# Sparse attention feeding a squared-ReLU MLP on one core: batches 2 to 4 loaded by casting DMAs with long rows, their local q and k transposed on TensorE

## The chip, the cores and the metric

The kernel runs on one core of a Trainium2 chip. A core has TensorE (PE: matmuls, with its weight loads shown as PEld), VectorE (DVE), ScalarE (ACT), GpSimd (POOL), and SyncE (SP), which here only issues DMAs. The metric is the device time of one execution in microseconds; several executions are taken and their median is given.

## What is computed

Attention over 8 batches of 8 heads, 576 positions and 64 channels. Heads 0 to 3 are local (a query sees itself and the 31 positions before it), heads 4 to 7 are strided (it sees earlier positions with the same remainder modulo 32). The result, with heads side by side, is a matrix of 4608 tokens by 512, and goes through an MLP with a squared ReLU:

```python
scores = scale * np.matmul(q, k.transpose(0, 1, 3, 2))
scores = np.where(masks[None, :, :, :], scores, -1000000000.0)
attn = np.exp(scores - np.max(scores, axis=-1, keepdims=True))
attn = attn / (np.sum(attn, axis=-1, keepdims=True) + 1e-09)
x = np.matmul(attn, v).transpose(0, 2, 1, 3).reshape(B * S, H * D)
...
r = np.maximum(x @ w_in, 0.0)
return (r * r) @ w_out
```

## The kernel before

**Work and tiles.** The unit of attention is a pair of heads of one batch: unit u is batch u // 4, pair u % 4; the first two pairs are local, the last two strided. A local unit needs only band blocks (96 queries against 128 keys), a strided one only the blocks of equal remainder (72 by 72). All operands of TensorE are bf16. The attention result is kept transposed in four tiles `xt`, [128 channels, 4608 tokens]. The MLP works on nine chunks of 512 tokens. For a chunk c, `mm1(c, ff)` is four 512-column matmuls into a "ph" bank, a Relu on ACT (L478) and a square on DVE (L481) into `g_sb`; `mm2(c, i)` is four 512-column matmuls (L495) of the second product, and every fourth one copies a finished [128, 512] tile (L499) and stores it through SP (L503). PSUM has eight banks: two "ph", one "py", five "pt".

**Steps of a unit.** T (`step_T`, L284) transposes local q or k on TensorE, six 96-column products, and copies q on ACT (L297) and k on DVE (L299). S (`step_S`, L333) makes the scores into four "pt" banks; ACT exponentiates them bank by bank (L343), DVE multiplies by the 0/1 mask (L349). Without `at_once` the four exponentials and two masks are spread over the next ticks, one per group, by `later`. D (`step_D`, L418) multiplies by V, whose 65th column of ones gives the sum, and DVE divides (L430, L431); a local unit has two parts, a strided one three. E (`step_E`) brings x into `xt`: by a DMA transpose on SP for local units from batch 2 on (L441), else by TensorE transposes (L448) and a copy (L454, L456). Batches 0 and 1 have their own forms for strided units: TS transposes q and k on TensorE (L186), N sums over keys by a product with ones (L381), O multiplies by V and DVE scales into `xt` (L394, L396).

**Order.** The schedule is written by hand. `first_steps` does batch 0 and the first five products of chunk 0. Then a list of groups is built, one group being one `mm1` or one `mm2` quarter: groups 0 to 15 chunk 0 first product (0 to 4 are empty), 16 to 31 its second product, 32 to 47 `mm1(1)`, 48 to 63 `mm2(1)`, 64 to 79 `mm1(2)`, and from 80 on `mm1(c)` and `mm2(c - 1)` in turn, 32 groups per chunk. Batch 1's steps are hung on groups 12 to 31 by `second(n, ...)`. The steps of batches 2 to 7 stand in one list (`stream_steps`), and `due` spreads each batch's steps over a stretch of groups in proportion to `weights`: batch 2 ends at group `ready[2]` = 56, batch b from 3 on at `starts[b]`, the first group of chunk b. A step that is due is issued ahead of its group on every engine, so each engine's queue is in this order, and an instruction that waits holds up all behind it on its engine.

**Loads.** Batches 0 and 1 and the weights come by casting DMAs issued from POOL (`load_qk_local_sw`, `load_v_local_sw`, `load_v_str_first`, `load_w_in`, `load_w_out`), which write bf16. From batch 2 on `loads(b)` issues on SP plain loads of local q and k (L118 for batches under `LB` = 4, else L112), local V (L210) and strided V (L242) in fp32, and POOL casts them (L140, L217, L218, L249). Strided q and k go by a casting DMA from POOL to DRAM (`cast_str_dram`, L163) and come back by a DMA transpose on SP (`transpose_str`, L171). For batches from `LB` on local q and k are transposed by DMA on SP too (`transpose_local`, L198) rather than by T. Batch 2's loads hang on group 18 and are held by a one-element POOL copy (L117) that reads the last part of `w_out_b`; batch 3's hang on group 34, and those of later batches are placed by `plan`. Staging tiles for q and k have two buffers each, the tiles for V four slots that batches use in turn.

The lines that fix the stretches and the loads of batches 2 and 3:

```python
weights.append(3 if c < 3 else 5)        # L688, mm1
weights.append(7 if c < 2 else 5)        # L691, mm2
ready = {2: 56}                          # L714
plan(2, 18, 0, 0)                        # L761
plan(3, 34, 0, 0)                        # L763
```

Of the kernel before, what the change touches and what calls it, by code (L numbers as in the profile page):

```python
# [14 lines left out]
def kernel(  # L15
# [18 lines left out]
    NJ = 8  # L34
# [67 lines left out]

    LB = 4

    def load_qk_local(u, eng, gate=None):
        b, p = units[u]
        s = st.setdefault(u, {})
        for name, src in (("q", q), ("k", k)):
            t = qk_st.tile([QL, 2, 6 * D], FP32, name=f"{name}_st")
            if b >= LB:  # L110
                for hh in range(2):
                    eng.dma_start(out=t[:, hh].rearrange("p (t d) -> p t d", d=D),  # L112
                                  in_=src[b, 2 * p + hh].rearrange("(t p) d -> p t d", p=QL))
                s[name + "f"] = t
                continue
            if gate is not None and name == "q":
                nc.gpsimd.tensor_copy(t[0:1, 0, 0:1], gate)  # L117
            eng.dma_start(out=t, in_=src[b, 2 * p:2 * p + 2]  # L118
                          .rearrange("h (p j) d -> p h (j d)", j=6))
            s[name + "f"] = t  # L120
# [35 lines left out]

    XB = 2
    big = {}

    def cast_str_dram(b):  # L160
# [7 lines left out]
    def transpose_str(b):  # L168
        for name in "qk":
            o = strT.tile([128, NJ // 2, 4 * SP_], BF16, name=f"{name}T_s")  # L170
            nc.sync.dma_start_transpose(out=o, in_=big.pop((b, name)))  # L171
            for i in range(2):
                st.setdefault(4 * b + 2 + i, {})[name + "T"] = o[:, :, 2 * SP_ * i:2 * SP_ * (i + 1)]
# [85 lines left out]

    clock = [0]  # L260
    pending = []

# [42 lines left out]
    def step_S(u, at_once=False):  # L305
# [57 lines left out]
        expo(0, 0)  # L363
        later(1, lambda: expo(0, 1), u)
        later(2, lambda: (masks(0), expo(1, 0)), u)
        later(3, lambda: expo(1, 1), u)
        later(4, lambda: masks(1), u)
# [66 lines left out]
    def step_E(u):  # L434
# [3 lines left out]
        local = is_local(u)  # L438
        n, w = (NL, QL) if local else (NJ, SP_)
        if local and b >= XB:  # L440
            nc.sync.dma_start_transpose(  # L441
                out=xt[p][:, b * S:(b + 1) * S].rearrange("c (t q) -> c t q", q=QL),
                in_=x.rearrange("p n d -> p (n d)"))
            st.pop(u)
            return
# [18 lines left out]
    def mm1(c, ff, kks=range(4), order=range(4), pool=None):  # L464
# [3 lines left out]
        if kks[0] == order[0]:  # L468
            phs[ff] = banks["pt"].pop(0) if pool == "pt" else bank(pool or "ph")
        ph = phs[ff]  # L470
# [8 lines left out]
        if c == 0 and 2 < ff < NP:  # L479
            banks["pt"].insert(0, ph)  # L480
        later(1, lambda: nc.vector.tensor_tensor(g[:, ff, :], r, r, op=ALU.mult))  # L481
# [3 lines left out]
    def mm2(c, i, pool=None):  # L485
        j, part = divmod(i, 4)
        g = gs[c]
        if part == 0:
            if pool == "pt":
# [15 lines left out]
    T_ = lambda u, nm: (lambda: step_T(u, nm))  # L505
    S_ = lambda u, at_once=False: (lambda: step_S(u, at_once))
    D_ = lambda u, part: (lambda: step_D(u, part))
# [34 lines left out]
    def stream_steps(lo, hi, base):  # L542
        order = [T_(lo, "q"), T_(lo, "k"), T_(lo + 1, "q"), S_(lo), T_(lo + 1, "k")]
        ends = {}
        for u in range(lo, hi + 1):
            if u < hi - 1:
                order.append(S_(u + 1))
            if u > lo:
                order.append(E_(u - 1))
                ends[u - 1] = base + len(order)  # L550
            if u < hi:
                order.append(D_(u, 0))
                if u + 2 < hi and has_T(u + 2):
# [9 lines left out]

    gates = {2: w_out_b[0:1, 12, 0:1]}

    def loads_1():
# [8 lines left out]
        load_w_out(3)  # L575
        for t in vl_sts:
            nc.gpsimd.memset(t[0:32], 0.0)

    def loads(b):
        u = 4 * b  # L580
        for i in range(2):
            load_qk_local(u + i, nc.sync, gate=gates.get(b) if i == 0 else None)
        for i in range(2):
            load_v_local(u + i, nc.sync)
        load_v_str(u + 2, nc.sync)
        load_v_str(u + 3, nc.sync)
        if b >= XB:
            cast_str_dram(b)
        cast_qk_local(u, pool2)
        cast_qk_local(u + 1, pool2)  # L590
        cast_v_local(u)
        cast_v_local(u + 1)
        cast_v_str(u + 2)
        cast_v_str(u + 3)

    def loads_qk(b):
        for i in range(2):
            load_qk_local(4 * b + i, nc.sync)
        cast_str_dram(b)
# [80 lines left out]
    def add(c, kind, i, pool=None):  # L680
# [3 lines left out]
        elif kind == 1:  # L684
            if i == 0:
                starts[c] = len(groups)
            groups.append(lambda: mm1(c, i))
            weights.append(3 if c < 3 else 5)  # L688
        else:
            groups.append(lambda: mm2(c, i, pool))  # L690
            weights.append(7 if c < 2 else 5)  # L691

# [6 lines left out]
    for part in range(4):  # L699
        for j, pool in ((0, "ph"), (1, "ph"), (2, None), (3, "pt")):  # L700
            add(0, 2, 4 * j + part, pool)
    mm1_alone(1)
    for i in range(16):
        add(1, 2, i, "ph")
# [8 lines left out]
    due = [0] * (len(groups) + 1)  # L713
    ready = {2: 56}  # L714
    hooks = {}
# [3 lines left out]

    def plan(b, n0, g0, g1):  # L720
        if b < LB:
            at(n0, lambda: loads(b))
            if b >= XB:
                at(n0 + (12 if b == 2 else 6), lambda: transpose_str(b))
            return
        g = g0 + (g1 - g0) * 45 // 100
        at(g, lambda: loads_qk(b))
        at(max(g + 8, g0 + (g1 - g0) * 8 // 10), lambda: transpose_str(b))
        at(n0, lambda: loads_v(b))
        for i in range(2):  # L730
            at(g + 14 + 4 * i, lambda u=4 * b + i: transpose_local(u))

# [9 lines left out]
    N_, O_ = (lambda u: lambda: step_N(u)), (lambda u: lambda: step_O(u))  # L742
    second(12, lambda: cast_qk_local(4, dve2, "q"))
    second(13, T_(4, "q"), lambda: cast_qk_local(4, dve2, "k"))
    second(14, T_(4, "k"), lambda: cast_qk_local(5, dve2, "q"))
    second(15, T_(5, "q"), lambda: cast_qk_local(5, dve2, "k"))
    second(16, T_(5, "k"))
    second(17, S_(4, True))
    second(19, S_(5, True))
    second(20, D_(4, 0))  # L750
    second(21, D_(4, 1), ts("q", 0))
    second(22, ts("q", 1), D_(5, 0))
    second(23, E_(4), D_(5, 1))
    second(24, ts("k", 0), ts("k", 1))
    second(25, E_(5))
    second(26, S_(6, True))
    second(28, S_(7, True), N_(6))
    second(29, O_(6))
    second(30, N_(7))
    second(31, O_(7))  # L760
    plan(2, 18, 0, 0)  # L761
    done_prev, g_prev = 0, 32
    plan(3, 34, 0, 0)  # L763
    for b in range(2, B):
        g_end, s_end = ready.get(b, starts[b]), ends[4 * b + 3]
        total = sum(weights[g_prev:g_end])
        for g in range(g_prev, g_end + 1):
            due[g] = done_prev + (s_end - done_prev) * sum(weights[g_prev:g]) // total
        if b + 2 < B:
            plan(b + 2, g_end + 2, g_prev, g_end)  # L770
        done_prev, g_prev = s_end, g_end
    done = 0
    for n, g in enumerate(groups):
        while done < due[n]:
            steps[done]()
            done += 1
# [36 lines left out]
```

The softmax here doesn't subtract the row's maximum and nothing guards it: scores larger than these inputs give would overflow.

## Time and profile before

| | |
|---|---|
| median of 8 runs | 319.03 us (318.19 to 319.97) |
| profiled execution, its own time | 319.91 us |
| span of its trace | 318.2 us |
| granted TensorE clock | 0.999 |
| DMA, mean over the span | 136 GB/s, 43.41 MB |
| hardware queue (SP), share of 16 engines | 44.5% |
| software queue (POOL), share | 23.0% |

The costliest groups of instructions, as the page gives them (busy time in us, then the mean of one in ns):

| line | engine, what | count | busy | mean |
|---|---|---|---|---|
| L472 | PE, first product | 549 | 141.5 | 379 |
| L495 | PE, second product (py and ph) | 534 | 137.1 | 379 |
| L478 | ACT, Relu | 141 | 84.0 | 598 |
| L481 | DVE, square | 144 | 67.3 | 469 |
| L343 | ACT, exponential | 128 | 48.0 | 407 |
| L431 | DVE, scale of x | 68 | 36.0 | 509 and 554 |
| L349 | DVE, mask | 56 | 30.6 | 588 and 504 |

How to read it: a matmul's duration (379 ns) is longer than the distance to the next one, since matmuls are pipelined, so PE's busy share overstates and its holes are found from start times. Some matmul records are missing (549 of 564 L472 rows into "ph"). In the rows of slices a digit is the busy share in tenths of one fortieth of the span, 7.95 us. In the chain of waits each piece is what released the next one, from the last instruction back. Idle time of ACT, DVE or POOL costs nothing by itself.

### The profile page before, as it was taken

The numbers are of one execution on the slowest core, as the hardware profiler recorded it, in microseconds if no ns is written. First come the engines' busy times: TensorE is split into PE (matmuls) and PEld (weight loads), VectorE is DVE, ScalarE is ACT, GpSimd is POOL, SyncE is SP. The second block draws the span as 40 slices with busy tenths as digits, with TensorE's granted clock in tenths as the row PEclk, the third lists the DMA queues.
The fourth block names the chain that finished last, engine by engine and source line by source line (L and its number), as shares of the span: only waits on it lengthen the run. The fifth ranks groups of instructions, "written<-read, shape, count | busy, mean of one in ns | idle before, by whom it ended". The sixth has DMA issues, their size and how long they took to land.

```text
span 318.2 us, 6089 instructions
## 1 busy us (share of the span) xinstructions
PE 300.4 (94%) x2319; PEld 148.4 (47%) x2362; DVE 163.4 (51%) x398; ACT 164.5 (52%) x339; POOL 83.1 (26%) x108
## 2 busy tenths in 40 slices
PE   8899699989899989999999999999999999999994
PEld 3544354444455444444444444544444444444441
DVE  5366653569766875755565557464455222222200
ACT  3757455777446765554555455545543344444311
POOL 8653213718820822831363024000000000000000
PEclk9999999999999999999999999999999999999999
DMA  8999979999998997998796575100421100000121
GB/s 158 164 205 205 190 132 261 214 255 221 235 143 195 190 248 170 240 191 209 182 216 146 139 180 99 39 25 31 54 66 50 37 33 35 33 33 35 52 80 66
DMA packets 87052, 43.41 MB, mean 136 GB/s; under 512 B 72112, under 2 KB 79984, under 8 KB 86832
## 3 DMA queue, kind: packets, MB, share of 16 engines
q1 hardware_dynamic: 73520, 31.86, 44.5%
q0 software_dynamic: 13504, 11.17, 23.0%
q8 instruction: 18, 0.29, 0.4%
q14 instruction: 10, 0.08, 0.1%
HBM read 37.08 MB, written 12.98 MB: 157 GB/s over the span
## 4 chain that ended last, share of the span: by engine, by line
PE 88%; DVE 5%; ACT 3%; issue 2%; ACTq 0%; DVEq 0%
PE ph L472 35%; PE py L495 27%; PE ph L495 10%; PE pt L418 4%; PE pt L333 4%; PE py L514 2%; ACT r L478 2%; PE pt L448 1%; DVE xt L456 1%; PE pt L495 1%; ACT e L343 1%; PE pt L284 1%; DVE g_sb L481 1%; DVE e L349 1%; DVE kTl L299 1%
## 5 line engine op out<-in xcount | busy, mean ns | idle before, releaser
L472 PE MATMUL ph<-xt,w_in_b 128*128 128x512 bf16 x549 | 141.5, 379 | 3.3 <-DVE xt L456 1.9
L478 ACT ACTIVATE r<-ph 128x512 bf16<-128x512 f32 x141 | 84.0, 598 | 100.3 <-PE ph L472 95.7
L481 DVE TENSOR_TENSOR g_sb<-r 128x512 bf16<-128x512 bf16 x144 | 67.3, 469 | 105.8 <-ACT r L478 105.3
L495 PE MATMUL py<-w_out_b,g_sb 128*128 128x512 bf16 x380 | 99.7, 379 | 1.6 <-issue 0.6
L495 PEld LDWEIGHTS <-g_sb 128*128 128x128 bf16 x576 | 52.8, 98 | 60.4 <-issue 3.1
L472 PEld LDWEIGHTS <-w_in_b 128*128 128x128 bf16 x576 | 51.6, 98 | 54.0 <-issue 0.8
L343 ACT ACTIVATE e<-pt 72x288 bf16<-72x288 f32 (+1 forms) x128 | 48.0, 407 | 14.6 <-PE pt L333 14.4
L495 PE MATMUL ph<-w_out_b,g_sb 128*128 128x512 bf16 x154 | 37.4, 379 | 0.3
L418 PEld LDWEIGHTS <-e 128*128 128x128 bf16 (+1 forms) x384 | 20.1, 97 | 15.6 <-issue 1.9
L217 POOL CAST vl<-vl_st 128x768 bf16<-128x768 f32 x12 | 10.6, 887 | 48.1 <-DMA vl_st<-in_v_dram 36.1
L349 DVE TENSOR_TENSOR e<-e,mask_str 72x576 bf16<-72x576 bf16 x28 | 16.5, 588 | 5.7 <-ACT e L343 5.5
L431 DVE TENSOR_TENSOR x_s<-pt,rinv 72x384 bf16<-72x384 f32 (+1 forms) x36 | 18.3, 509 | 1.2
L431 DVE TENSOR_TENSOR x_l<-pt,rinv 96x384 bf16<-96x384 f32 x32 | 17.7, 554 | 1.1
L430 DVE RECIPROCAL rinv<-pt 96x6 f32<-96x6 f32 (+2 forms) x68 | 12.6, 185 | 9.4 <-PE pt L418 9.1
L140 POOL CAST q_l<-q_st 96x768 bf16<-96x768 f32 x12 | 11.4, 954 | 20.6 <-DMA q_st<-in_q_dram 20.0
L499 ACT COPY y<-py 128x512 f32<-128x512 f32 x25 | 14.6, 585 | 4.0 <-PE py L495 4.0
L140 POOL CAST k_l<-k_st 96x768 bf16<-96x768 f32 x12 | 10.9, 909 | 15.7 <-DMA k_st<-in_k_dram 14.4
L349 DVE TENSOR_TENSOR e<-e,mask_full 128x576 bf16<-128x576 bf16 x28 | 14.1, 504 | 1.7 <-ACT e L343 1.5
L499 ACT COPY y<-ph 128x512 f32<-128x512 f32 x10 | 5.8, 584 | 17.1 <-PE ph L495 17.1
L249 POOL CAST vs<-v_st 72x1024 bf16<-72x1024 f32 x12 | 13.7, 1165 | 1.0 <-DMA v_st<-in_v_dram 0.6
L418 PE MATMUL pt<-vs,e 72*128 72x65 bf16 x192 | 11.9, 193 | 1.2 <-ACT e L343 1.1
L418 PE MATMUL pt<-vl,e 128*128 128x65 bf16 x192 | 10.7, 193 | 0.0
(100 smaller groups left out, 171.5 us busy)
## 6 DMA issues: line engine op xcount, KB each, us to landing
out_dram<-y SPq DMA_DIRECT2D x36, 256.0 KB, 2.4
vl_st<-in_v_dram SPq DMA_DIRECT2D x24, 144.0 KB, 3.1
v_st<-in_v_dram SPq DMA_DIRECT2D x12, 288.0 KB
q_st<-in_q_dram SPq DMA_DIRECT2D x16, 144.0 KB, 6.5
k_st<-in_k_dram SPq DMA_DIRECT2D x16, 144.0 KB, 5.9
w_out_b<-in_moe_w_out_dram POOLq DMA_DIRECT2D x4, 512.0 KB, 14.4
q_d<-in_q_dram POOLq DMA_DIRECT2D x6, 288.0 KB, 5.2
k_d<-in_k_dram POOLq DMA_DIRECT2D x6, 288.0 KB, 6.4
```

The source lines that it names most:

```text
L140: copy(t.rearrange("p j h d -> p h j d"), s[name + "f"].rearrange("p h (j d) -> p h j d", j=6))
L249: (copy or nc.gpsimd.tensor_copy)(t[:, :, 0:D], s["vf"].rearrange("p h (j d) -> p (h j) d", d=D))
L333: nc.tensor.matmul(pss[row][half][0:kn, w * i:w * (i + 1)], lhsT, rhs, start=u > 3, stop=True, skip_group_check=u < 4)
L343: nc.scalar.activation(e[0:kn, lo:lo + S // 2], pss[row][half][0:kn, 0:S // 2], AF.Exp, scale=scale)
L349: nc.vector.tensor_tensor(x, x, m, op=ALU.mult)
L418: nc.tensor.matmul(po[:, n - n0, :], e[0:kn, pos(n):pos(n) + 128], rhs[0:kn, src(n), 0:D + 1], start=True, stop=True)
L431: nc.vector.tensor_tensor(x, po[0:w, 0:m, 0:D], rinv[0:w, 0:m].to_broadcast([w, m, D]), op=ALU.mult)
L472: nc.tensor.matmul(ph, w_in_b[:, kk, 128 * ff:128 * (ff + 1)], xt[kk][:, 512 * c:512 * (c + 1)], start=(kk == order[0]), stop=(kk == order ...
L478: nc.scalar.activation(r, ph, AF.Relu)
L481: later(1, lambda: nc.vector.tensor_tensor(g[:, ff, :], r, r, op=ALU.mult))
L495: nc.tensor.matmul(py, g[:, ff, 128 * j:128 * (j + 1)], w_out_b[:, ff, :], start=(ff == 0), stop=(ff == 15))
L499: nc.scalar.copy(y, py)
```

## The change

It has these parts.

- *Loads of batches 2 to 4.* `loads(b)` and its gate are gone. Local q and k of both local units come by one casting DMA each from POOL (`load_qk_local_sw`, four heads, 1536-byte rows), and DVE rearranges them (`cast_qk_local(u, dve2, ...)`). Local V comes by casting DMAs into the V tile, behind a one-element POOL copy that reads the transposed strided k of the same batch (`load_v_local_gated`). Strided V comes by four casting DMAs straight into its tile (`load_v_str_direct`). They hang on groups 14, 29, 43 and 65.
- *`LB` 4 to 5.* Batch 4's local q and k are transposed by T instead of by DMA. The loads of batch 5 on SP get a gate on batch 4's strided V.
- *Strided x of batches 6 and 7* (`XD`): to DRAM by SP, and back into `xt` by a DMA transpose, instead of TensorE transposes and a DVE copy.
- *Order in a unit.* The staged exponentials run in the order of their banks, (0,0), (1,0), (0,1), (1,1); D's first part stands ahead of E of the unit before; an empty step is put into the head of the list.
- *Stretches.* New weights; batch 2 ends at group 58, batches 3 to 5 two groups before their chunk, 6 and 7 fourteen before. In groups 48 to 62 scores are exponentiated at once (`relaxed`).
- *Batch 1* one to four groups earlier; the two POOL memsets of the V staging tiles move from the end of `loads_1` to group 50.
- *PSUM.* The first products ff = 5 to 7 of chunk 0 use "pt" banks.
- *End.* The last 128 tokens are made in two halves of 256 columns, each with its own copy and store.

In the built program POOL issues 60 DMAs instead of 36 and has 30 casts fewer, SP has the plain loads of batches 2 to 4 and four local transposes fewer, four DRAM stores and four DMA transposes more; DVE has 12 q and k copies more and two k copies (`kTl`) more, and 4 copies into `xt` fewer.

```diff
-    LB = 4
+    LB = 5
...
+            if gate is not None and name == "q":
+                nc.gpsimd.tensor_copy(t[0:1, 0, 0:1], gate)
...
+    XD = B - 2
+    came = {}
...
             nc.sync.dma_start_transpose(out=o, in_=big.pop((b, name)))
+            came[b] = o[0:1, 0, 0:1]
...
-        later(1, lambda: expo(0, 1), u)
-        later(2, lambda: (masks(0), expo(1, 0)), u)
-        later(3, lambda: expo(1, 1), u)
+        later(1, lambda: expo(1, 0), u)
+        later(2, lambda: expo(0, 1), u)
+        later(3, lambda: (masks(0), expo(1, 1)), u)
...
+        if not local and b >= XD:
+            xd = dram.tile([S, 2 * D], BF16, name="x_d")
+            nc.sync.dma_start(out=xd.rearrange("(p j) c -> p (j c)", j=NJ), in_=x.rearrange("p n d -> p (n d)"))
+            nc.sync.dma_start_transpose(out=xt[p][:, b * S:(b + 1) * S], in_=xd)
+            st.pop(u)
+            return
...
-            phs[ff] = banks["pt"].pop(0) if pool == "pt" else bank(pool or "ph")
+            phs[ff] = banks["pt"].pop(0) if pool == "pt" else bank(pool[:2] if pool else "ph")
...
-            banks["pt"].insert(0, ph)
+            banks["pt"].append(ph)
...
+        if c == NCH - 1 and j == 3:
+            if part % 2:
+                return
+            cols = slice(128 * part, 128 * part + 256)
+            py = bank(pool)[:, 0:256]
+            for ff in range(16):
+                nc.tensor.matmul(py, g[:, ff, 128 * j:128 * (j + 1)], w_out_b[:, ff, cols],
+                                 start=(ff == 0), stop=(ff == 15))
+            y = y_pool.tile([128, 512], FP32, name="y")
+            nc.scalar.copy(y[:, 0:256], py)
+            r0 = 512 * c + 128 * j
+            nc.sync.dma_start(out=out[r0:r0 + 128, cols], in_=y[:, 0:256])
+            return
...
-    S_ = lambda u, at_once=False: (lambda: step_S(u, at_once))
+    S_ = lambda u, at_once=False: (lambda: step_S(u, at_once or relaxed[0]))
...
+            if u < hi:
+                order.append(D_(u, 0))
             if u > lo:
                 order.append(E_(u - 1))
                 ends[u - 1] = base + len(order)
             if u < hi:
-                order.append(D_(u, 0))
...
+    def load_v_local_gated(b):
+        nc.gpsimd.tensor_copy(vl_all[64:65, (2 * b) % NV, 0, 0, 0:1], came[b])
+        load_v_local_sw(b)
+
+    def load_v_str_direct(b):
+        for u in (4 * b + 2, 4 * b + 3):
+            t = vss[v_slot(u)]
+            h = 2 * units[u][1]
+            for i in range(2):
+                nc.gpsimd.dma_start(out=t[:, NJ * i:NJ * (i + 1), 0:D],
+                                    in_=v[b, h + i].rearrange("(p j) d -> p j d", j=NJ))
+            st.setdefault(u, {})["v"] = t
...
-            load_qk_local(4 * b + i, nc.sync)
+            load_qk_local(4 * b + i, nc.sync, vss[v_slot(4 * b - 1)][0:1, NBS - 1, 0:1] if b == LB and i == 0 else None)
...
-            groups.append(lambda: mm1(c, i))
-            weights.append(3 if c < 3 else 5)
+            groups.append(lambda: mm1(c, i, pool="pt free" if c == 0 and i < NP + 3 else None))
+            weights.append(4 if c == 1 else 3 if c < 3 else 5)
...
-            weights.append(7 if c < 2 else 5)
+            weights.append(6 if c < 2 else 5)
...
-    ready = {2: 56}
+    ready = {2: 58, **{b: starts[b] - (14 if b >= XD else 2) for b in range(3, B)}}
...
+            at(g0, lambda: transpose_str(b))
+            for i in range(2):
+                at(g1 + 2 * i, lambda u=4 * b + i: cast_qk_local(u, dve2, "q"))
+                at(g1 + 2 * i + 1, lambda u=4 * b + i: cast_qk_local(u, dve2, "k"))
...
+    second(10, lambda: cast_qk_local(4, dve2))
+    second(11, lambda: cast_qk_local(5, dve2))
+    second(12, T_(4, "q"), T_(4, "k"))
...
+    rows = lambda b: (lambda: load_qk_local_sw(b, (4 * b, 4 * b + 1)))
+    second(14, rows(2), lambda: cast_str_dram(2))
+    plan(2, 28, 28)
+    second(29, lambda: load_v_local_gated(2), lambda: load_v_str_direct(2), rows(3), lambda: cast_str_dram(3))
+    plan(3, 42, 46)
+    second(43, lambda: load_v_local_gated(3), rows(4), lambda: load_v_str_direct(3), lambda: cast_str_dram(4))
+    plan(4, 64, 62)
+    second(65, lambda: load_v_local_gated(4), lambda: load_v_str_direct(4))
+    for t in vl_sts:
+        second(50, lambda t=t: nc.gpsimd.memset(t[0:32], 0.0))
```

## The prediction

> **What bounds the kernel now.** I read the busy shares first, then the rows of 40 slices, then a table of stages cut at the borders of the group list.
>
> ```profile
> PE 300.4 (94%) x2319; PEld 148.4 (47%) x2362; DVE 163.4 (51%) x398; ACT 164.5 (52%) x339; POOL 83.1 (26%) x108
> PE   8899699989899989999999999999999999999994
> DMA  8999979999998997998796575100421100000121
> ```
>
> ```profile
> 25.80:38.60 12.80, 9.64 (x62) 4.57 (x62) 7.88 (x25) 7.64 (x14) 4.41 (x6) 1.00 1.49 196
> 38.60:59.80 21.20, 19.85 (x217) 10.32 (x219) 10.70 (x24) 12.41 (x30) 6.22 (x9) 1.00 0.96 209
> 79.20:100.20 21.00, 19.39 (x222) 10.77 (x226) 14.10 (x37) 10.38 (x26) 8.72 (x10) 1.00 1.00 193
> 246.50:318.20 71.70, 67.38 (x308) 30.51 (x312) 13.59 (x32) 25.66 (x44) 0.00 (x0) 1.00 0.12 45
> ```
>
> In the table the columns after the length are the busy times of PE, PEld, DVE, ACT and POOL, then the granted clock. TensorE is the bound: the clock is granted in full, and from 246.5 us on it runs without a hole, so ending attention sooner adds nothing by itself. What can be won is holes before that. A matmul's recorded time overlaps the next one, so I took starts from the timeline instead: in unbroken runs 512-column matmuls start 0.216 us apart (four in 0.86 us in the chain), 96-column transposes 0.042, 65-column products 0.030. Whatever lies between two starts beyond that is a hole. Holes over 0.13 us sum to 3.60 us in A (25.8 to 38.6, first product of chunk 0), 2.12 in B (to 59.8, its second product), 1.50 in C (to 79.2, chunk 1 first), 3.15 in D (to 100.2, chunk 1 second), 1.28 in E (to 118.2, chunk 2 first), then 0.91, 0.91, 0.91 and 0.36 per batch: 14.7 us. Some 0.09 us on each side of every score step is the price of switching; it stays.
>
> The chain of waits says who made the holes of A:
>
> ```profile
> 26.07 0.65 ACT r L478
> 31.91 0.43 DVE g_sb L481
> 32.33 1.33 DVE q_l L140
> 36.10 0.67 DVE kTl L299
> 36.77 0.28 DVE q_l L140
> ```
>
> ```profile
> 32.01 1.43 POOL L577 MEMSET vl_st<- 32x768 f32 x2
> 32.25 1.41 DVE L140 COPY q_l<-q_st 96x768 bf16<-96x768 bf16 x1
> 76.10 1.01 POOL L140 CAST k_l<-k_st 96x768 bf16<-96x768 f32 x1
> 76.35 1.84 DVE L349 TENSOR_TENSOR e<-e,mask_str 72x576 bf16<-72x576 bf16 x1
> ```
>
> The second four are from the timeline. A copy that takes 0.35 us elsewhere takes 1.41 while a POOL memset runs; a mask product of 0.44 us takes 1.84 among POOL casts. Such stretched DVE operations add up to 6 us in 62 to 110 us, just where D has its holes.
>
> **Part by part.**
>
> A. The three first products whose PSUM went through the two "ph" banks get "pt" banks: the hole at 25.84 (0.71 us, PE waiting for ACT's backlog of five Relus) goes. The casts of batch 1 move from groups 12 to 15 to groups 10 and 11, and the POOL memsets leave for group 50: the holes at 31.73 (1.77) and 35.75 (1.12) go. Late next are ACT, which still has its backlog when the q copies (0.64 us each) come, and the staging loads: issued at 14.05 and 15.98 us with 13.6 and 12.6 to landing, they are there at 28.6, and group 10 starts at about 28.7. I keep 0.5 us for both: 3.6 - 0.5 = 3.1 us won (bounds 2.0 and 3.6).
>
> B. The same steps one group earlier, the sums of unit 6 no longer in the group of unit 7's scores (holes 0.52 and 0.47 at 53), no POOL casts beside DVE; but four DVE casts of batch 2 (4 x 0.35) in the last four groups. Half of 2.12: 1.1 us won (0.2 to 1.9).
>
> POOL and queues. Batches 2 to 4 lose 12 of L140's casts, six of each of L217 and L218 and six of L249 on POOL (11 + 5.3 + 5.1 + 7.0 = 28 us), and their SP loads; DVE gets 12 copies (4.2 us). Instead POOL issues 24 more DMAs (36 to 60). Here a rule speaks against the change.
>
> ```profile
> 63.95 0.49 POOL L163 DMA_DIRECT2D q_d<-in_q_dram  x1
> 20.70 0.73 POOL L235 DMA_DIRECT2D vl<-in_v_dram  x1
> ```
>
> ```profile
> DMA packets 1697, 1.58 MB, mean 197 GB/s; under 512 B 163, under 2 KB 1696, under 8 KB 1696
> DMA packets 2042, 0.27 MB, mean 133 GB/s; under 512 B 2035, under 2 KB 2042, under 8 KB 2042
> ```
>
> The rows say an issue costs POOL 0.5 to 1.3 us with DVE busy beside it. The Trainium skill (SBUF — State Buffer, "SBUF: two separate sides") warns that descriptors of POOL-issued DMAs can't be written while DVE holds the shared port in a fast mode, and gives 620 ns growing to 3100; DVE's masks, squares and new casts would be that. By the rule 24 issues cost 60 us more, 20 per batch, and the loads are late (rival 1); by the rows about 20 us in all, less than the casts taken away. I take the rows: every DVE operation here is under 0.8 us when alone. The last two lines are the DMA view for 36 to 44 and for 10 to 12 us: POOL's queue alone moves 0.197 MB/us in long pieces, 0.133 in pieces of 128 bytes. So one q or k transfer (0.295 MB) takes 1.5 us, a batch's local V (3040 pieces) about 3, its strided V (2304, now in 128-byte pieces too) 2.3.
>
> Do they arrive? The queue runs dry at 45 us today (the gate on batch 2 opened at 46.1). Batch 2's four q/k transfers follow directly: rows landed by 49, DRAM copies by 52 (two at 2 us), two DMA transposes issued in 1.3 to 3 us and landed in some 4.3 each: 58. The new gate makes POOL wait for them; behind it on POOL stand V of batch 2, then batch 3's rows and DRAM copies. V lands at 62, strided V at 65. First use: the product of unit 8 at group 41, about 66 us in the faster kernel. Each further batch repeats this in 19 to 20 us, PE needs 21: V of 3 at 82 for 87, V of 4 at 101 for 108. Slack 3 to 7 us: cost nothing, while it holds. Casts at group 28 find rows there at 49 for 50.5; the SP transposes at groups 28, 42 and 64 stand before outputs only, which have four buffers. The gate for batch 5 holds SP's loads until strided V of 4 has landed, near 105, where they start at 110 today.
>
> C and D. Batch 2 has 58 instead of 56 groups and weights of 4 and 6, not 3 and 7: about 1 step a group in C and 1.5 in D, where D had 2. Scores in D are exponentiated at once. In C nothing lightens ACT (16 Relus of 0.60, some 13 exponentials of 0.41, two copies: 16.3 of some 17.5 us): 0.4 of 1.50 won (-0.5 to 1.2). In D the POOL contention is gone and the packing eased, but the memsets are now at group 50: up to 1.1 us, as at 32 us. 1.6 of 3.15 won (0.3 to 2.8).
>
> E. Batch 3 gets 20 groups instead of 24, and holds batch 4's four local transposes: 22 steps for 18. Four transposes of 0.26 us are 1.0 us more PE; DVE has per group 0.43 for a square and 0.85 steps of 0.64 us, 0.97 of some 1.0 us. That is at the limit: I charge 0.8 us of new holes (0 to 3). The 1.28 us hole at the end goes, because the batch must now be done two groups before its chunk:
>
> ```profile
> 117.10 0.68 DVE xt L456
> ...
> 149.19 0.77 DVE xt L456
> ```
>
> So do the four like the second line (0.36 each): 1.28 + 1.44 = 2.7 us (2.2 to 2.7).
>
> Exponentials in bank order: the second bank is free one tick after the first instead of two. It pays where a product takes that bank next, and is in C to E.
>
> Batches 6 and 7. Strided x goes to DRAM and comes back transposed: 4 x 8 transposes of 0.032 us leave PE, 1.0 us won, and 4 DVE copies. The round trip (2.4 us, then 4.4, as rows of similar DMAs) lies before chunk 6 and 7 by 14 groups, 12 us. SP waits inside it for the write; V of batch 7 is issued before. Batch 6 has 18 steps in 20 groups instead of 32: DVE 0.75 of 1.0 us a group. Nothing charged (0 to 1).
>
> Tail.
>
> ```profile
> 314.27 0.58 ACT L499 COPY y<-ph 128x512 f32<-128x512 f32 x1 [2.87 <-PE ph L495]
> 314.88 0.33 SPq L503 DMA_DIRECT2D out_dram<-y  x1
> ```
>
> The last copy has 256 columns (about 0.37 us, as L343's 288) and half the bytes follow: 0.4 us won (0.1 to 0.8). 32 matmuls of half width are the same columns.
>
> Sum: 3.1 + 1.1 + 0.4 + 1.6 - 1.0 - 0.8 + 2.7 + 1.0 + 0.4 = 8.5 us. The span falls from 318.2 to 309.7; with the 1.7 us around it (319.91 - 318.2) 311.4. The profiled execution is 0.9 over the median 319.03, so 310.5 by the median. I say **311.0**.
>
> **Rivals.** (1) *V or rows come late, slower than before.* Place: products of units 8, 12 and 16. Three rounds of the chained queue start at 45 us; the third V must land by 108. At c us a round it lands at 45 + 3c; the 8.5 us are gone at c = 23.8 against my 19 to 20. With the rule's 2.5 us on three of ten issues a round c = 27, the third V lands at 126, 18 us late: 329. For it: slack is 3 us at batch 2 and the rounds are in series. Against: loads no longer compete with SP's.
>
> (2) *DVE takes PE's place in C to E.* It has some 44 us of work in 53; at 0.97 in E each late step holds a bank. If C and D keep their holes (2.0 us) and E gets 3 instead of 0.8, 4.2 us go: 315.2. For it: E's sum. Against: no stretched operations remain before batch 5.
>
> (3) *All holes up to 118 us go* (11.6 us won there instead of the 6.7 that A to E come to after the charge on E): 306. Against: B and C have ACT at its limit.
>
> (4) *The change does nothing in sum*, data late by what holes give: 319.
>
> Chances: forecast 0.50 (its own range 309 to 313.5), rival 2 0.23, rival 3 0.13, rival 1 0.10, rival 4 0.04. A measurement can tell 0.3%, 1 us. Faster 0.86, within 0.04, slower 0.10. The range leaves out rivals 1 and 4 and the far half of rival 3: 306.0 to 317.5.
>
> **What would show it.** A: no hole over 0.5 us between 25 and 35, the DVE copy of batch 1's q at 0.35 us. D: DVE mask products all near 0.44 us. Boundaries: no PE wait on the DVE copies into xt. E: holes on DVE's drains. A PE wait at a local product (L422) for a DMA into vl, or a DVE cast waiting for q_st, is rival 1; POOL issues above 2 us are the rule. I am wrong if C to E take over 57 us.

## The result, and the profile after

The changed kernel takes 314.56 us (median of 11 runs, 311.94 to 315.88), the one before 319.19 in the same series: a ratio of 0.985, 95% interval 0.9829 to 0.9871. It is 1.5% faster where 311.0 us, 2.6% less, was forecast. Medians in this text count every execution; ratios leave out the three that took over 1.5% more than the fastest of their kernel, one each in e1, e4 and e5. The profiled execution took 314.34 us for a span of 312.6.

The page of the changed kernel, its busy shares and the rows for TensorE and its granted clock:

```profile
span 312.6 us, 6073 instructions
PE 299.3 (96%) x2329; PEld 150.0 (48%) x2370; DVE 157.1 (50%) x408; ACT 164.7 (53%) x342; POOL 75.5 (24%) x105
PE   7889999989999999699999999999999999999995
PEclk9999999999999999989999999999999999999999
```

TensorE's row has one dark slice, the 17th (125 to 133 us), and the clock, flat before, has a digit below 9 in the next one. A table of stretches of the same trace there, cut where the clock changes (length, busy PE, PEld, DVE, ACT, POOL, granted clock, DMA share, GB/s):

```profile
128.57:131.98 3.41, 1.00 (x15) 0.59 (x16) 0.78 (x3) 0.41 (x1) 2.04 (x3) 1.00 0.95 192
131.98:135.40 3.42, 3.42 (x15) 1.46 (x14) 1.11 (x3) 1.20 (x3) 2.44 (x4) 0.50 1.03 214
135.40:138.81 3.41, 3.41 (x29) 1.76 (x28) 2.06 (x6) 1.50 (x3) 0.49 (x1) 1.00 0.65 139
```

TensorE stands for 2.4 us of the first stretch and is busy all through the second, but with half its clock: 3.42 / 2 = 1.7 us of work are lost there without any idle time. Hole and clock together cost some 4 us.

What released it is in the chain of waits (start, length, what):

```profile
121.08 0.57 SPq L213
...
125.72 5.22 DMA kTl<-k_l
130.94 0.05 issue
130.99 0.43 PE pt L337 x12
```

The scores of unit 20, the first of batch 5, wait for the DMA transpose of its k. Back along SP's queue and POOL's, in the timelines of the two:

```profile
99.93 0.18 POOL L600 COPY vl<-kT_s 1x1 bf16<-1x1 bf16 x1 [14.53 <-DMA kT_s<-k_d]
101.09 1.21 POOL L237 DMA_DIRECT2D vl<-in_v_dram  x1 [0.97 <-PE pt L458]
103.03 3.24 POOL L608 DMA_DIRECT2D vs<-in_v_dram  x4
109.78 0.18 POOL L111 CAST q_st<-vs 1x1 f32<-1x1 bf16 x1 [3.51 <-DMA vs<-in_v_dram]
```

```profile
109.99 0.89 SPq L114 DMA_DIRECT2D q_st<-in_q_dram  x2
```

POOL opens the gate of batch 5 (L111) when strided V of batch 4 has landed, at 109.8 us, and SP's loads of batch 5 start at 110.0. In the kernel before, the same loads started at 109.9. TensorE has got ahead of them: chunk 3 starts at 110.76 instead of 116.08.

To see where the time went, I take the starts of certain weight loads in both traces (all 576 records of them are there), which divide the span at the first product of a chunk. "Mended" is the version of run e7 below, in which the hole is gone:

| stretch | before | after | forecast | measured | mended, against before |
|---|---|---|---|---|---|
| A, from group 5 to the second product of chunk 0 | 14.32 | 11.19 | -3.1 | -3.1 | -3.1 |
| B, to chunk 1 | 21.15 | 19.30 | -1.1 | -1.9 | -1.9 |
| C and D, to chunk 2 | 40.41 | 39.44 | -2.0 | -1.0 | -1.0 |
| E, to chunk 3 | 16.08 | 16.69 | +1.8 | +0.6 | +0.6 |
| chunk 3 to chunk 4 | 32.88 | 36.18 | -1.3 | **+3.3** | -0.7 |
| chunk 4 to chunk 8 | 123.42 | 120.55 | -2.4 | -2.9 | -2.9 |
| chunk 8 to the end | 45.82 | 45.11 | -0.4 | -0.7 | -0.6 |
| span | 318.2 | 312.6 | -8.5 | -5.6 | -9.5 |

(The forecast's 1.28 us hole stands in the row from chunk 3 on, since it came just after chunk 3's first product.) All rows but one are within 1.2 us of the forecast, and that one misses by 4.6.

### The profile page after: what moved, and what is told of

It is laid out like the page before. It is cut to its first block, busy times and chain, and to the rows that moved or that the text cites. A ratio compares the mean times of both kernels' runs of the same rounds, so it can differ in the third digit from the quotient of the medians.

```text
span 312.6 us, 6073 instructions
## 1 busy us (share of the span) xinstructions
PE 299.3 (96%) x2329; PEld 150.0 (48%) x2370; DVE 157.1 (50%) x408; ACT 164.7 (53%) x342; POOL 75.5 (24%) x105
## 4 chain that ended last, share of the span: by engine, by line
PE 90%; DMA 3%; issue 2%; ACT 1%; DVE 1%; POOL 1%; SPq 1%; POOLq 0%; ACTq 0%
PE ph L482 37%; PE py L518 27%; PE ph L518 10%; PE pt L337 4%; PE pt L422 4%; DMA kTl<-k_l 2%; PE pt L482 1%; PE pt L288 1%; DMA vl_st<-in_v_dram 1%; PE ph L504 1%; PE pt L518 1%; PE pt L458 1%; ACT e L347 1%; SPq L173 1%; PE pt L398 1%
## 5 line engine op out<-in xcount | busy, mean ns | idle before, releaser
L482 PE MATMUL ph<-xt,w_in_b 128*128 128x512 bf16 x533 | 138.6, 381 | 1.5 <-issue 0.8
L488 ACT ACTIVATE r<-ph 128x512 bf16<-128x512 f32 x138 | 82.4, 598 | 98.3 <-PE ph L482 94.4
L491 DVE TENSOR_TENSOR g_sb<-r 128x512 bf16<-128x512 bf16 x144 | 64.5, 448 | 110.4 <-ACT r L488 109.4
L518 PE MATMUL py<-w_out_b,g_sb 128*128 128x512 bf16 x385 | 101.7, 382 | 1.0 <-issue 0.3
L518 PEld LDWEIGHTS <-g_sb 128*128 128x128 bf16 x560 | 51.0, 98 | 55.2 <-issue 1.3
L347 ACT ACTIVATE e<-pt 72x288 bf16<-72x288 f32 (+1 forms) x128 | 45.4, 407 | 12.0 <-PE pt L337 12.0
L518 PE MATMUL ph<-w_out_b,g_sb 128*128 128x512 bf16 x141 | 34.3, 379 | 0.3 <-issue 0.2
L522 ACT COPY y<-py 128x512 f32<-128x512 f32 x25 | 14.6, 586 | 7.0 <-PE py L518 6.5
L353 DVE TENSOR_TENSOR e<-e,mask_str 72x576 bf16<-72x576 bf16 x28 | 13.5, 494 | 4.3 <-ACT e L347 4.2
L220 POOL CAST vl<-vl_st 128x768 bf16<-128x768 f32 x6 | 5.1, 851 | 30.6 <-DMA vl_st<-in_v_dram 19.0
L337 PEld LDWEIGHTS <-kT_s 64*72 64x72 bf16 x256 | 6.0, 113 | 7.8 <-issue 7.4
L608 POOL DMA_DIRECT2D vs<-in_v_dram x12 | 9.7, 818 | 0.0
```

The lines of the kernel that those rows point to most:

```text
L337: nc.tensor.matmul(pss[row][half][0:kn, w * i:w * (i + 1)], lhsT, rhs, start=u > 3, stop=True, skip_group_check=u < 4)
L347: nc.scalar.activation(e[0:kn, lo:lo + S // 2], pss[row][half][0:kn, 0:S // 2], AF.Exp, scale=scale)
L353: nc.vector.tensor_tensor(x, x, m, op=ALU.mult)
L482: nc.tensor.matmul(ph, w_in_b[:, kk, 128 * ff:128 * (ff + 1)], xt[kk][:, 512 * c:512 * (c + 1)], start=(kk == order[0]), stop=(kk == order ...
L488: nc.scalar.activation(r, ph, AF.Relu)
L518: nc.tensor.matmul(py, g[:, ff, 128 * j:128 * (j + 1)], w_out_b[:, ff, :], start=(ff == 0), stop=(ff == 15))
```

## The experiments

Each is the changed kernel with the edit shown. Ratios are against the kernel before; the changed kernel's own is 0.985 (0.9829 to 0.9871).

**e1: no gate.**

```diff
-            load_qk_local(4 * b + i, nc.sync, vss[v_slot(4 * b - 1)][0:1, NBS - 1, 0:1] if b == LB and i == 0 else None)
+            load_qk_local(4 * b + i, nc.sync)
```

> The changed kernel (314.6 us) without the gate that holds SP's loads of batch 5 until strided V of batch 4 has landed; the order on every engine stays. Theory (the gate makes batch 5's q and k late; TensorE stands 2.4 us before the scores of unit 20 and then runs some 4 us at half clock): loads start near 98 instead of 110 us, no hole over 0.5 us between 120 and 140, granted clock 0.999 or more, 310.6 us. Rival A (the loads then compete with V of batch 4, and the hole moves to the product of unit 16): a hole of 1 to 3 us near 107, 312 to 315. Rival B (the wait is the queue of DMA transposes on SP, whatever the loads do): the hole stays, 314.6.

Measured: 312.28 us, ratio 0.9782 (0.9742 to 0.9821). Loads start at 98.3 us and no hole stands before unit 20. But rival A came true as well: in the profiled execution (315.23 us) TensorE waits 1.6 and 1.8 us at unit 16's product. A piece of the chain of waits, and the stretch in which the clock fell:

```profile
102.89 8.43 DMA vl<-in_v_dram
```

```profile
110.92:114.33 3.41, 2.98 (x19) 1.60 (x19) 0.91 (x3) 0.80 (x2) 0.82 (x1) 0.50 1.71 212
```

V's second transfer takes 8.43 us from issue to landing, where it took 5.2 in the changed kernel: batch 5's loads now run beside it. The clock falls to half again, for 3.4 us. So the gate does protect V of batch 4, and the price of V being late is paid in the same way. The mechanism is confirmed, the expected 310.6 isn't reached.

**e2: the third round earlier.**

```diff
-    plan(4, 64, 62)
+    plan(4, 60, 62)
```

> The changed kernel with the gate, but the DMA transposes of batch 4's strided q and k hung on group 60 instead of 64, so that on SP they stand ahead of two stores less. Theory: V of batch 4 lands and the gate opens some 3 to 4 us earlier; the hole before unit 20 shrinks to under 0.5 us, the clock stays up, 310.6 to 311.5. If the gate is not what decides, 314.6.

Measured: 310.94 us, ratio 0.9735 (0.9711 to 0.9759), as expected. Its trace does not show why: the profiled execution is its slowest (314.38 us; the six others took 310.39 to 311.54), the transposes stand only 1 us earlier there (93.85 instead of 94.91), and a hole of 3.0 us is still before unit 20. What the faster executions did was not seen. In e7 below, which contains this edit, the transposes are issued from 91.76 and no hole is left before unit 20.

**e2b: matmuls in the hole.** At the head of unit 20's scores:

```diff
+        if u == 20:
+            pw = bank("pt")
+            for _ in range(8):
+                nc.tensor.matmul(pw, idle[:, 0:128], idle, start=True, stop=True)
```

> The changed kernel with eight more 512-column matmuls (1.7 us, results not used) ahead of the scores of unit 20, where TensorE stands for 2.4 us. Theory (the idle stretch itself lowers the granted clock, which costs 1.6 us): the hole becomes 0.7 us of idle time, the clock is 0.999 or more, 313.0 us. Rival (the lower clock has nothing to do with the hole): clock stays at 0.995, 314.6 or, where the hole is short, up to 316.

Measured: 312.87 us, ratio 0.9799 (0.9769 to 0.983); the hole in its trace is 0.57 us, and the clock was 0.998 or more in all six runs (0.994 or 0.995 in seven of the changed kernel's eleven). Adding 1.7 us of useless work makes the kernel 1.7 us faster, at the very edge of what the two intervals can tell apart. Times and clocks agree, and so the clock's share of the loss is shown.

**e3: the gate reads local V.** Local V's last transfer stands before strided V in POOL's queue.

```diff
-... vss[v_slot(4 * b - 1)][0:1, NBS - 1, 0:1] if b == LB and i == 0 ...
+... vls[v_slot(4 * b - 4)][0:1, 0, 1, 0:1] if b == LB and i == 0 ...
```

> The changed kernel with the gate of batch 5's loads reading local V of batch 4 instead of strided V, the last thing in POOL's queue. Theory (the gate opens 2.4 us or more too late because four small-piece transfers of strided V stand before it): loads start near 106 instead of 110 us while local V has already landed, no hole before unit 20 and none at unit 16, clock 0.999, 310.6 us. Rival (any SP traffic in 100 to 110 us delays something that TensorE needs): a hole over 1 us stays somewhere between 100 and 135, 312 to 315.

Measured: 311.33 us, ratio 0.9744 (0.972 to 0.9768). Most runs are at 310.4 to 311.4. In the profiled one (313.34) V of batch 4 was late (holes of 1.2 and 1.1 us at unit 16) although no load of SP ran beside it, so the third round has no slack in some executions. There the gate opened no earlier than in the changed kernel (SP's loads started at 110.57), and 0.73 us of hole was left before unit 20: what was expected of this trace failed. None of the three holes lowered the clock. The faster executions were not traced.

**e7: both.** The edits of e2 and e3 together.

> Both mends together: the gate of batch 5's loads on local V of batch 4, and the DMA transposes of batch 4's strided q and k hung on group 60. Theory (the two act on the same chain, whose last link is late by some 2 to 4 us; either is enough in most executions): no wait at unit 16 or unit 20, 310 to 310.8, no more than 0.8 us better than either alone. If they were independent losses, 308 to 309.

Measured: 310.37 us (310.36 to 310.97), ratio 0.9732 (0.9708 to 0.9756), the best of the study and, over four executions, the steadiest. The two mends act on one chain, as expected: they don't add. The gate in POOL's timeline, SP's first load after it, and four microseconds in which the changed kernel stood:

```profile
106.35 0.18 POOL L111 CAST q_st<-vl 1x1 f32<-1x1 bf16 x1 [2.08 <-DMA vl<-in_v_dram]
```

```profile
106.55 0.89 SPq L114 DMA_DIRECT2D q_st<-in_q_dram  x2
```

```profile
126.00:130.00 4.00, 4.00 (x34) 1.88 (x32) 2.01 (x6) 2.06 (x4) 3.30 (x4) 1.00 0.98 219
```

Opening the gate 3.4 us earlier removes 4.0 us from the stretch between chunks 3 and 4 (36.18 to 32.20). The only holes over 0.25 us left in this trace are two in C.

**e4 and e8: strided V by long rows.** On top of e3, strided V of batches 2 to 4 comes by one transfer with 1024-byte pieces into a staging tile, and DVE spreads it.

```diff
-    ... lambda: load_v_str_direct(2) ...
+    ... lambda: load_v_str_rows(2) ...
+    second(40, lambda: cast_v_str(10, nc.vector.tensor_copy), lambda: cast_v_str(11, nc.vector.tensor_copy))   # e8: 47
```

and likewise for batch 3 (e4 at group 56, e8 at 62) and 4 (76, 83). `load_v_str_rows` only calls `load_v_str_sw`, the form with one transfer.

> As the run with the gate on local V, and strided V of batches 2 to 4 comes in one transfer of long rows into a bf16 staging tile and is spread by two DVE copies per batch, in place of four transfers of 128-byte pieces. Theory (POOL's issue of 0.81 us per small transfer and 2304 pieces a batch make the rounds long): V of batches 2 to 4 is there 2 to 4 us earlier, POOL has 9.7 us less of issues; six DVE copies of some 0.4 us are added where DVE isn't the bound: 310 to 311. Rival (DVE is at its limit in C to E): 312 to 313.

> As the run with long rows of strided V, with the DVE copies hung on groups 47, 62 and 83 instead of 40, 56 and 76. Theory (there DVE stood 2 to 2.5 us before each pair of copies because V had not landed yet; the copies themselves cost 0.8 us of DVE a batch): no DVE wait for v_st, 310 to 311.5. Rival (the long-row transfer itself delays the rows of the next batch): 313 or more.

Measured: e4 317.57 us, ratio 0.9941 (0.9916 to 0.9966); e8 311.24, ratio 0.9763 (0.9737 to 0.9789). In e4 I hung the copies too early; DVE's timeline shows it standing, with masks and drains queued behind:

```profile
67.12 0.76 DVE L252 COPY vs<-v_st 72x1024 bf16<-72x1024 bf16 x2 [2.50 <-DMA v_st<-in_v_dram]
```

The transfer, issued at 60.24, landed at 67.1, where the forecast's sum has strided V at 65. TensorE then stood 2.55 us at a product that waited for one of these masks, and the clock fell here too. Hung later, the same code is level with e3. That alone would say little, since e3 has hardly a wait left to remove; but in e8's trace strided V of the three batches lands at 66.3, 90.7 and 109.5 us, in the changed kernel's, in four transfers, at 66.0, 90.2 and 109.7. So the small pieces aren't what makes the rounds long, against my expectation.

**e5: strided x on TensorE.**

```diff
-        if not local and b >= XD:
+        if not local and b >= B:
```

> As the run with the gate on local V, but strided x of batches 6 and 7 is transposed on TensorE and copied by DVE as before the change (32 transposes of 0.032 us). The forecast's term: 1.0 us slower than that run, 311.6. Rival (the round trip through DRAM costs SP and DMA what it saves PE): the same time.

Measured: 313.25 us, ratio 0.9806 (0.9776 to 0.9837), 0.6% slower than e3; the intervals just miss each other. In its trace chunk 5 to chunk 8, where the two x are made, takes 89.78 us against 88.73 in e7's: 1.05 more, the forecast's 1.0. The other large loss in it is a hole of 1.22 us before unit 20, which has to do with the gate and not with x.

**e6: batches 3 to 5 end at their chunk.**

```diff
-    ready = {2: 58, **{b: starts[b] - (14 if b >= XD else 2) for b in range(3, B)}}
+    ready = {2: 58, **{b: starts[b] - (14 if b >= XD else 0) for b in range(3, B)}}
```

> As the run with the gate on local V, but batches 3 to 5 end at the first group of their chunk instead of two groups before it, as they did before the change. The forecast's term: three of the five holes at the borders come back, one of up to 1.28 and two of 0.36 us, 1.0 to 2.0 us slower than that run, 311.6 to 312.6. Rival (stretching batch 3 by two groups eases E by as much): the same time.

Measured: 314.56 us, ratio 0.9863 (0.9837 to 0.989), 3.2 us slower than e3. The holes at the borders of chunks 3, 4 and 5 are 1.06, 1.45 and 1.07 us in its trace, where the kernel before had 1.28, 0.36 and 0.36: with the new order they would be larger. Two groups of lead are worth 3.6 us in sum, where I had counted 2.0 for these three, and the expected 311.6 to 312.6 is missed.

**e9: memsets early.** On top of e3, the POOL memsets are back at the end of `loads_1`.

> As the run with the gate on local V, but the two POOL memsets are back at the end of the first loads (near 32 us) instead of group 50. Theory (their harm in A was that they fell on the q cast, which now runs earlier): no hole over 0.3 us in A; DVE squares near 32 us stretched to about 1 us; D loses its 1.4 us of POOL; same time within 0.6 us. Rival (they stop DVE whatever it does, and PE after it): 1.0 us slower, with a hole near 33.

Measured: 311.61 us, ratio 0.9766 (0.9732 to 0.98), the same as e3 within the intervals. A has no hole. My expectation of stretched squares fails: the square that starts within POOL's second memset (31.88 to 33.31 us) keeps its length, and so does the copy out of PSUM beside the first one.

```profile
31.59 0.75 DVE L303 COPY kTl<-pt 128x576 bf16<-128x576 bf16 x1
31.88 1.43 POOL L599 MEMSET vl_st<- 32x768 f32 x2
32.61 0.43 DVE L491 TENSOR_TENSOR g_sb<-r 128x512 bf16<-128x512 bf16 x1 [0.27 <-ACT r L488]
```

So in A the earlier casts do it, and the memsets could have stayed.

**e10: the old order of exponentials.** On top of e3, the three `later` lines as before the change.

> As the run with the gate on local V, with the staged exponentials back in the order (0,0), (0,1), (1,0), (1,1). Theory (the bank that a product takes next is then freed a tick later): 0.5 to 1.5 us slower, new holes before products in E and after. Rival (ACT is behind by more than a tick in C, and not behind elsewhere, so the order doesn't matter): same time within 0.5 us.

Measured: 310.77 us, ratio 0.974 (0.9716 to 0.9764), level with e3. The order of the banks brings nothing that can be told here.

**e11: the old weights.** On top of e7, 3 and 7 for batches 2 and 3 as before the change.

> Both mends (gate on local V, transposes on group 60), and the group weights of batches 2 and 3 as before the change: 3 for every first product of chunks 1 and 2, 7 for a second-product quarter, so that chunk 1's first product carries fewer steps and its second product more. With the mends alone the only holes left over 0.35 us are two of 0.82 and 0.90 us in C, both before score products while ACT stood in exponentials. Theory (in C ACT is at its limit: 16 Relus of 0.60 us and 13 exponentials of 0.41): the two holes in C shrink to under 1 us in sum, and D, with two steps a group, gets holes of 0.5 to 1.5 us; the time is 310.0 to 311.5. Rival (D has room now that POOL's casts are gone): 309.0 to 309.8.

Measured: 310.68 us, ratio 0.9737 (0.9715 to 0.9758). C takes 17.03 us instead of 19.97 and has no hole, D 23.00 instead of 19.48, with five holes of 0.44 to 0.58 us. The two weights move 3 us between C and D, and the sum changes by 0.6.

## Why the prediction was right or wrong

**Right.** The sign, and the reason: TensorE is the bound and holes ahead of 250 us are what can be won. A came out to a tenth, at -3.1: the q copy of batch 1 on DVE, 1.41 us before, is now

```profile
29.84 0.35 DVE L140 COPY q_l<-q_st 96x768 bf16<-96x768 bf16 x1
```

and TensorE has no hole over 0.25 us in A. That the number fits to a tenth is luck in part: all 3.60 us of A's holes went, and the 0.5 that I had kept back is not a wait but the scores of unit 4, which moved from B into A. The borders between chunks are clean, as the step "the batch must now be done two groups before its chunk" said; e6 shows that it is worth 3 us for batches 3 to 5. The round trip of x is worth 1.0 us (e5). The rule against POOL-issued DMAs was rightly set aside: POOL's 12 issues of strided V take 0.81 us each with DVE at work, not 3.1, and no issue behind 44 us takes over 1.53. The 60 us were an estimate from the page's two figures. Stretched DVE operations are gone from 25 to 117 us: the first over 0.12 us too long in that part of the changed kernel's trace starts at 117.7, when POOL casts batch 5.

**Wrong: the slack, and the gate of batch 5, costed at nothing.** The step was "Slack 3 to 7 us: cost nothing, while it holds", with the remark that the gate "holds SP's loads until strided V of 4 has landed, near 105, where they start at 110 today". Three errors are in it.

The first is the length of the rounds. Besides the copy at 99.93 shown above, POOL's copies that start V's transfers ran at

```profile
56.10 0.18 POOL L600 COPY vl<-kT_s 1x1 bf16<-1x1 bf16 x1 [17.54 <-DMA kT_s<-k_d]
75.51 0.18 POOL L600 COPY vl<-kT_s 1x1 bf16<-1x1 bf16 x1 [11.15 <-DMA kT_s<-k_d]
```

These are rounds of 19.4 and 24.4 us, where I had 19 to 20. The copy waits for the DMA transposes of strided q and k, which I had placed "before outputs only". Those on group 64 stood on SP behind two transposes of x and a store, from 89.89 to 94.81; in e7, on group 60, they are issued from 91.76, ahead of these, and the copy runs at 97.88. From the copy to the landing of strided V it then took 9.8 us, to 109.7. My 5.3 us were for moving the pieces, which took 5.9 (103.0 to 108.9); the wait for TensorE (0.97), the issues in series ahead of them and the landing behind them were not in the sum. V of batch 4 was forecast "at 101 for 108". Its local part, issued at 102.29 with 5.2 us to landing, was there at 107.5 for a product at 107.9, and in e3's trace not even that.

The second is the comparison. I held the gate's time against the start of these loads in the kernel before, not against their use. The scores of unit 20 started at 138.5 before and are due at 128.6 now, 9.9 us earlier, so loads at 110 are late though they start no later than they did. I had worked out first uses for V of batches 2, 3 and 4, and none for q and k of batch 5.

The third I had not seen at all: the way from these loads to the landing of k grew from 14.6 us (109.9 to 124.5) to 21.0 (110.0 to 130.9). On SP the loads of batch 5's V now stand ahead of unit 20's transposes; they stood behind. First the kernel before, then the changed one:

```profile
122.11 1.22 SPq L198 DMA_TRANSPOSE kTl<-k_l  x1
123.39 3.31 SPq L210 DMA_DIRECT2D vl_st<-in_v_dram  x4
```

```profile
121.08 2.22 SPq L213 DMA_DIRECT2D vl_st<-in_v_dram  x4
125.72 1.22 SPq L201 DMA_TRANSPOSE kTl<-k_l  x1
```

The new stretches put V's loads on group 80 and the transposes on 81, where they were 82 and 80. The transpose of k is issued 3.6 us later for it, and takes 5.2 us to land instead of 2.4. Before, k was there 14.0 us ahead of its use; 9.9 and 6.4 us together are 2.3 more than that, about the hole of 2.4. By an estimate from these rows, with V's loads (121.08 to 124.32) behind the transposes k would land some 3.3 us sooner, at 127.6, in time although the gate opens at 109.8. No run tried this order. e3 and e7 show that an earlier gate is enough, e1 that dropping it moves the wait to V of batch 4.

**Wrong: the price of a hole.** The forecast counts a hole at its length. This one costs 4.0 us at a length of 2.4; the rest is half of the 3.4 us at half clock (e2b).

**Rivals, and luck.** The mechanism of rival 1 (data late, rounds in series) was the right one, at a place I hadn't named and at less than its price. Rival 2 didn't happen: E grew by 0.6 us for 1.0 us more of transposes, with no hole over 0.25 us. So it is chance that the measured 314.56 lies next to rival 2's 315.2, and that it falls in 306.0 to 317.5 is due to the width that rivals 2 and 3 gave this range; it lies outside the forecast's own 309 to 313.5. My sign of being wrong, "C to E over 57 us", came true, but only just: from the first product of chunk 1 to the second of chunk 2 it was 58.2 us before and is 57.4 now. It was set in the wrong place, 0.3 us above my own terms (58.2 - 2.0 + 1.8 - 1.3 = 56.7), while the loss lay behind E, where I had set no sign.

Without the hole the sum is -9.5 against my -8.5. That E cost 1.2 us less, B won 0.8 more (0.5 of it the scores that went to A) and the tail 0.2 more outweighs C and D, which won 1.0 less. The step from 310.5, the sum by the median, to 311.0 is left without a reason.

**Mis-sized terms.** C was to win 0.4 and D 1.6, but C takes 1.98 us more (17.99 to 19.97) and D 2.94 less (22.41 to 19.47): the weights move steps between them, and only the sum of -1.0 is a gain. C's two holes of 0.82 and 0.90 us are in the traces of nearly all these kernels; in the changed kernel's chain:

```profile
63.56 0.22 ACT r L488
...
64.02 0.41 ACT e L347
...
64.48 0.28 PE pt L337 x5
```

The scores wait for exponentials that stand behind Relus on ACT. That ACT is at its limit in C was in the forecast; that C would be given more steps as well was there too, and I should have put both into one number. The tail was to win 0.4 and won 0.71 (from the start of the last copy to the end of the span, 3.91 to 3.20 us): 0.21 in the copy, the rest after it.

## What to carry to other kernels

When a kernel gets faster in one stage, every load with a fixed or inherited start becomes later by as much: set the time of each arrival against its first use in the new schedule, for the first stage that was not changed too. When groups or stretches move, read again in which order each queue now stands: by the estimate above, two groups of transfers that changed places cost as much here as the late gate. A gate that keeps transfers apart should wait for the last thing it protects, not for the last thing in the queue. Costs of groups in a hand-written schedule move work between stages, so neighbouring stages that share them are to be summed before a gain is claimed.

## What the runs showed of the hardware

- Not every hole lowers the clock, and its length alone does not say which. In the changed kernel 2.4 us of hole were followed by half clock, in e2's trace 3.0 us were not. Counted from where the clock first comes up, every stretch at full clock that ends within a trace is a whole number of 3.41 us long (in the changed kernel 126.29 us, 37 of them, before the fall), and each of the three falls ahead of the last 10 us lasts 3.41 us, 1.7 us of lost work. So I cut the traces into stretches of 3.41 us from that point (5.69 us in the changed kernel). Those in which TensorE was busy least, the tails aside:

| trace | stretch | TensorE busy in it | clock in the next |
|---|---|---|---|
| e1 | 107.51 to 110.92 | 0.75 | 0.50 |
| changed kernel | 128.57 to 131.98 | 1.00 | 0.50 |
| e4 | 64.47 to 67.89 | 1.41 | 0.50 |
| e2 | 129.96 to 133.38 | 1.61 | 1.00 |
| kernel before | 31.04 to 34.45 | 1.75 | 1.00 |
| e3 | 108.58 to 111.99 | 1.91 | 1.00 |

In all 14 traces, tails included, the clock fell after each such stretch in which TensorE was busy for 1.41 us or less, and after none with 1.60 or more. e2's hole was spared since it lay across two stretches, 1.2 us of it in one and 1.8 in the other. The Trainium skill (TensorE: Matmul & The Clock Gate, "Part 1: The HAM clock gate") gives half rate after an idle window of about 3.4 us that runs free of the kernel. The window agrees with these traces; that it must be idle throughout does not.

- A POOL memset stretched a DVE copy from SBUF to SBUF from 0.35 to 1.41 us in the kernel before, but neither a DVE product of two SBUF tiles (0.43, e9) nor a copy out of PSUM (0.75, e9). Among POOL casts, which read SBUF, a mask product took 1.84 us instead of 0.44 in the kernel before. The Trainium skill (SBUF — State Buffer, "Who interferes with whom") separates the same cases: for a product of two SBUF tiles only a POOL operation that reads SBUF is to matter, and such a product has no fast mode. So of the masks, squares and casts that the prediction counted as fast-mode operations only the casts could be that.
